# Attention B's output projection: the last group's rows stacked high, high, low for three of four blocks, with its loads moved

## The chip, the core and the metric

The kernel runs on one core of one Trainium2 chip. The time is device microseconds (us) of one launch, from the host's arrays in DRAM to the finished output in DRAM. A shorter time is better.

## The reference, cut to what matters

Two independent attentions, A and B, over S = 2048 positions with D = 576 and 32 heads of Dh = 18 columns each. Their outputs stand side by side, 2048 x 1152.

```python
qkv = x @ wqkv                                   # both A and B, separate weights
# A: each position sees 8 positions, two apart, itself and backwards; softmax; times v
# B: full softmax attention over all 2048 positions
scores = einsum("bhqd,bhkd->bhqk", q, k) * Dh**-0.5
o = einsum("bhqk,bhkd->bhqd", softmax(scores), v)
B = o.transpose(0, 2, 1, 3).reshape(1, S, D) @ wo   # the sum that is changed here
out = concatenate([A, B], axis=-1)
```

What the change touches is the last line for B: 2048 x 576 times 576 x 576, in float32 accuracy.

## The kernel before

**Numbers in halves.** TensorE multiplies in a reduced float32 form here. To keep the accuracy, an operand is kept as a rounded high part and the rest, a low part, and a product is the sum of three: high times high, high times low, low times high. Where the contraction is short, the three products are one instead: the rows are stacked (high, high, low against high, low, high), so that one matmul of 3 x 18 = 54 rows does what three of 18 rows do. The scores of B are made in that way in both kernels (`stack_loads`, line 132).

**B's attention.** The 32 heads are 8 groups `g` of four heads, the 2048 query positions 4 blocks `b` of 512, and the keys 16 tiles `kt` of 128. The main loop (line 1220) takes 8 x 4 x 16 = 512 steps. A step makes the scores of four heads (line 269), their exponentials on ScalarE (line 277), and adds the products with v into the PSUM tile `po` (`weigh`, line 742), one step later. Between these, TensorE makes the maxima of later blocks (line 158), which VectorE reduces (line 166). The maxima of a whole block are turned and written by eight small DMAs (`place`, line 195) into two rows of that block's `qs` tile: `qs<-mh` four times and `qs<-mt` four times. The first score of a block can't start before these have landed. The four maxima of a step run out near step 488 of 512.

**Order.** There is no scheduler: every engine works its instructions in the order in which this Python text issues them. `agenda` maps a step to the functions that are run at its end (`later`, `plan`, `due`, lines 105 to 117). All loads and stores of this stage go through `load`, which is SyncE's (SP's) one DMA queue, in order. In the built program each DMA also waits for the DMA eight places before it in the queue, since eight semaphores are used in turn; so at most eight are under way.

**After a block (`finish`, line 747).** `po` is copied to `o`, its denominators travel to `den`, are inverted on VectorE (line 782), travel back spread out as `rec`, and GpSimd (POOL) multiplies, rounds and subtracts (lines 785 to 787) to get the high and low parts. For groups 0 to 6 these are stored to the DRAM tensor `do`. For group 7, block 0 does this over 26 steps into the tiles `at0` and `at1`; blocks 1 and 2 do it within a few steps with transposes on VectorE instead (`shortly`, line 791); block 3 ends the kernel (`closing`, line 822).

**B's projection.** The weights `wo` of B are five chunks: four of 126 rows, which are 7 heads of groups 0 to 6 each, and one of the four heads of group 7, at rows 0, 32, 64 and 96 of its tile (lines 1151 and 842). Each chunk has a high and a low part. `fetch_old(b)` (line 1011) loads the old rows of block `b`, groups 0 to 6, from `do`: eight DMAs of 252 KB. `full(b, new)` (line 1122) then plans eight quarters: 128 positions times half of the 576 columns. A quarter (`sum_of`, line 1079) runs two rows of sums beside each other, on rows 0 to 63 and 64 to 127 of the array, in two PSUM tiles: five chunks times three products, so 15 pairs of matmuls, 64 x 288 each (line 1071). Quarters go into `inside` (within a step that still has maxima) or `waiting` (between steps). `partial` (line 1138) makes 12 pairs, the old rows only, for three quarters of the positions of block 3.

**Attention A** runs on POOL and VectorE beside the steps (`local`, line 864). Its last outputs, four of them, each go through `together` (line 1175), which does two steps in one with A's projection between (line 1193). Its loads are `at<-dao`, `ahl<-dao` and `aq<-dao`, its stores `dao<-aohi` and `dao<-ao`.

**Steps of group 7** start at 448. There `load_wo` for B's five chunks is planned at 7, 9, 11, 13, 15 (names `y<-wob`; POOL splits each three steps later), `fetch_old(0)` at 4, `fetch_old(1)` at 11, `fetch_old(3)` at 34 and `fetch_old(2)` at 38.

Of the kernel before, what the change touches and what calls it, by code (L numbers as in the profile page):

```python
# [7 lines left out]
F32 = mybir.dt.float32  # L8
F32R = mybir.dt.float32r
# [7 lines left out]
S = 2048  # L17
D = 576
H = 32
DH = 18  # L20
W = 8
DIL = 2
NG = H // 4
NT = S // 128
NB = S // 512
# [4 lines left out]
SUB = AB // 4  # L30
HALO = DIL * (W - 1)

STEPS = NB * NT
# [15 lines left out]
def ap(t, *dims):  # L49

    return bass.AP(tensor=t.tensor, offset=t.offset, ap=[list(t.ap[0])] + [list(d) for d in dims])


def rows(t, *dims):

    return bass.AP(tensor=t.tensor, offset=t.offset, ap=[list(d) for d in dims])
# [3 lines left out]
def two_attentions(ctx: ExitStack, tc, xa, wa, woa, xb, wb, wob, out):  # L60
# [5 lines left out]
    nc = tc.nc  # L66
    load = nc.sync.dma_start

    const = ctx.enter_context(tc.tile_pool(name="const", bufs=1))
    dram = ctx.enter_context(tc.tile_pool(name="dram", bufs=1, space=DRAM))  # L70
# [19 lines left out]
    da = dram.tile([3 * D, HALO + S], F32, name="da")  # L90
    dao = dram.tile([NJ, 2, 4, D, SUB], F32, name="dao")
    drec = dram.tile([NG, NB, 4, 512], F32, name="drec")
    do = dram.tile([2, NG - 1, 128, S], F32, name="do")

    po = p_po.tile([128, 512], F32, name="po")

# [3 lines left out]
    def split_on(engine, hi, lo, raw):  # L100
        engine.tensor_copy(hi, raw)
        engine.tensor_sub(lo, raw, hi)
# [3 lines left out]
    step = 0  # L106

    def later(n, f):
        agenda[step + n].append(f)

    def plan(start, pieces):
        for n, f in pieces:
            agenda[start + n].append(f)
# [6 lines left out]
    sets = []  # L120
# [260 lines left out]
    with (tc.tile_pool(name="x", bufs=1, side="right") as xp,  # L381
# [103 lines left out]
        if True:  # L485
# [9 lines left out]
            chunks = [[(0, 0, 128)], [(0, 128, third - 128), (D, 0, 256 - third)], [(D, 256 - third, 128)]]  # L495
# [185 lines left out]
            for k in range(2, 14):  # L681
                n = 46 if k == 2 else 36 + 4 * k
# [64 lines left out]
    def finish(g, b):  # L747
        o = work.tile([128, 512], F32, name="o", bufs=2)
        if g == NG - 1 and b == NB - 1:
            return closing(b, o, work.tile([128, 512], F32, name="rec", bufs=1))  # L750
        if step + 1 in producing and total - sum(given) >= 8:
            leaving.append(lambda: nc.scalar.activation(o, po, AF.Copy))
        elif step + 1 in producing or sum(given) == total:
            nc.scalar.activation(o, po, AF.Copy)
        else:

            nc.vector.tensor_copy(o, po)
            copied.add(step + 1)
        den = work.tile([128, 16], F32, name="den", bufs=2)
        rec = work.tile([128, 512], F32, name="rec", bufs=1)  # L760
        parts = []

        def room():
            if g == NG - 1 and b == 0:

                parts[:] = [ap(work.tile([128, 4, 128], F32R, name=f"at{i}", bufs=1), (1, 512)) for i in range(2)]
            else:
                n = work.tile([128, 2, 512], F32R, name="n", bufs=1)
                parts[:] = n[:, 0], n[:, 1], n
            return parts  # L770

        if g == NG - 1 and b > 0:
            return shortly(b, o, rec, *room()[:2])

        def store():
            if g < NG - 1:
                load(do[:, g, :, 512 * b : 512 * b + 512].rearrange("i p n -> p i n"), parts[2].bitcast(F32))
            else:
                plan(step, full(b, parts))

        for at, f in ((1, lambda: load(den, o[DH:128:32])),
                      (8, lambda: nc.vector.reciprocal(den, den)),
                      (9, lambda: load(drec[g, b].rearrange("i (p n) -> (i p) n", n=16), den)),
                      (13, lambda: load(rec, rows(drec[g, b], (512, 4), (0, 32), (1, 512)))),
                      (20, lambda: nc.gpsimd.tensor_mul(o, o, rec)),
                      (21, lambda: nc.gpsimd.tensor_copy(room()[0], o)),
                      (22, lambda: nc.gpsimd.tensor_sub(parts[1], o, parts[0])),
                      (26, store)):
            later(at, f)

    def shortly(b, o, rec, hi, lo):

        def halved(cols):
            nc.gpsimd.tensor_copy(hi[:, cols], o[:, cols])
            nc.gpsimd.tensor_sub(lo[:, cols], o[:, cols], hi[:, cols])


        cols = [slice(256 * i, 256 * i + 256) for i in range(2)]
        apart = b == 1
        for i in range(2):  # L800
            later(1 + i * apart, lambda i=i: nc.vector.transpose(rec[:, cols[i]], o[:, cols[i]]))
        later(1 + 2 * apart, lambda: divided(rec))
        for i in range(2):
            later(1 + (3 + i) * apart, lambda i=i: nc.vector.transpose(o[:, cols[i]], rec[:, cols[i]]))
            later(1 + (3 + i) * apart, lambda i=i: halved(cols[i]))
        plan(step, [(at + 2, f) for at, f in full(b, (hi, lo))])

    def inverse(src, turned, cols, o):

# [32 lines left out]
    def load_wo(k, src, *pieces):  # L842

        raw = work.tile([128, D], F32, name="y", bufs=4)
        n = 0
        if len(pieces) == 4:
            nc.gpsimd.memset(raw, 0.0)
            n = 128
        for at, c0, m in pieces:
            load(raw[at : at + m], src[c0 : c0 + m])  # L850
            n = max(n, at + m)
        if k == "a":
            hi = work.tile([128, D], F32R, name="wohi", bufs=5)
            lo = work.tile([128, D], F32R, name="wolo", bufs=5)
        else:

            c = len(wo.get(k, []))
            hi, lo = (ap(t[:, 0, 0, :] if len(t.shape) == 4 else t[:, 0, :], (1, NB * 1024))[:, D * c : D * c + D]
                      for t in sets[(NG - 3) % 3])
        wo.setdefault(k, []).append((hi, lo))  # L860
        later(3, lambda: split_on(nc.gpsimd, hi[:n], lo[:n], raw[:n]))


    def local(j):
# [166 lines left out]
            olds[b].append([t[:n] for t in o])  # L1031


    sums = {}
    ys = {}

# [39 lines left out]
            rings["else"].append(rings["else"].pop(0))  # L1076
        return sums_

    def sum_of(y, t, h, chunks, kind=None):

        pos, cols = slice(128 * t, 128 * t + 128), slice(288 * h, 288 * h + 288)
        both = []
        for r in range(2):
            both.append([])
            for c, (hi, lo) in enumerate(chunks):
                at = slice(64 * r, min(64 * r + 64, hi.shape[0]))
                whi, wlo = wo["b"][c]
                both[r] += [(a[at, pos], w[at, cols]) for a, w in ((hi, whi), (hi, wlo), (lo, whi))]
        one, two = beside(kind, *both)
        if kind:  # L1090
            nc.vector.tensor_copy(y, one)
        else:
            nc.scalar.activation(y, one, AF.Copy)
        nc.vector.tensor_add(y, two, y)
# [24 lines left out]
            half_end(t, b, h, new)  # L1119
        load(out[512 * b + 128 * t : 512 * b + 128 * t + 128, D:], ys[t, b])  # L1120

    def full(b, new):
        def half(t, h):
            if total - sum(given) > 4:
                inside.append(lambda: quarter(t, h, "scores"))
            else:
                waiting.append(lambda: quarter(t, h))

        def quarter(t, h, *kind):
            if h == 0:  # L1130
                ys[t, b] = work.tile([128, D], F32, name="y", bufs=4)
            if h == 1:
                later(1, lambda: load(out[512 * b + 128 * t : 512 * b + 128 * t + 128, D:], ys[t, b]))
            sum_of(ys[t, b][:, 288 * h : 288 * h + 288], t, h, [*olds[b], new], *kind)

        return [(4 + 2 * t + h, lambda t=t, h=h: half(t, h)) for t in range(4) for h in range(2)]

    def partial(t, h):

        b = NB - 1  # L1140
        if h == 0:
            name = ("aq", "ao", "aohi")[t]
            ys["part", t] = work.tile([128, DH, SUB], F32, name=name, bufs=1)
        y = ap(ys["part", t], (1, DH * SUB))[:, 288 * h : 288 * h + 288]
        waiting.append(lambda: sum_of(y, t, h, olds[b]))
        sums[t, b, h] = (y,)

# [8 lines left out]
    for g in range(1, NG):  # L1156
        if g > EARLY:
            plan(STEPS * (g - 2) + 1, [(n, f) for n, f in enumerate(stack_loads(g))])
        if g == NG - 1:
            plan(STEPS * g, [(4, lambda: fetch_old(0)), (11, lambda: fetch_old(1)), (34, lambda: fetch_old(3)),  # L1160
                             (38, lambda: fetch_old(2))])
            plan(STEPS * g, [(n, lambda t=t, h=h: partial(t, h)) for n, (t, h) in
                             zip((43, 44, 45, 47, 49, 51), [(t, h) for t in range(3) for h in range(2)])])
            plan(STEPS * g, [(62, lambda: outside.append(lambda: first(3, NB - 1, 0)))])
            for b in range(NB - 1):
                producing.update(STEPS * g + NT * (b + 1) + (31 if b == 0 else 7) + n for n in range(8))
        plan(STEPS * (g - 1), [(24, lambda g=g: load_v(g))])

    ready = [(0, 0, 0, es)]
# [133 lines left out]
```

## Time and profile before

| | |
|---|---|
| median of 3 runs | 1602.95 us (1602.54 to 1606.55) |
| the profiled execution | 1601.25 us |
| its span in the profile | 1599.4 us |
| mean granted TensorE clock | 0.999 |
| TensorE busy (share of the span) | 1586.0 us (99%) |
| VectorE, ScalarE, GpSimd busy | 1363.5, 1214.4, 959.8 us |
| chain that ended last, TensorE's share | 90% |

The profile shows one execution. Times in it are us from the start of the span; the last step ends about 11 us before its end. PE is TensorE's matmuls, PEld its weight loads, DVE VectorE, ACT ScalarE, POOL GpSimd, SP SyncE. A row of a timeline gives the start, the time taken, the engine, the line of the kernel, the operation with output and input, the number of instructions that are merged in the row, and in brackets how long the engine had been idle before and what ended that. A row of windows gives the busy time of each engine within a stretch, then the granted clock, the mean share of the 16 DMA engines that was busy, and GB/s.

### The profile page before, as it was taken

The page shows a single profiled execution, that of the slowest core. Times are in us where ns is not written, and L with a number is a line of the kernel's source. Part 1 is how long each engine was busy: PE and PEld are TensorE (multiplying, and loading weights), DVE is VectorE, ACT ScalarE, POOL GpSimd, SP SyncE. Part 2 cuts the span into 40 slices and gives each one's busy share as a digit, 9 for nine tenths or more (in the row PEclk, how much of TensorE's full clock was granted, in tenths as well). Part 3 has the DMA queues.
Part 4 walks back from the last instruction along what each step waited for, and adds up shares of the span by engine and source line. Part 5 has one row for each costly group of instructions (what it writes and reads, how often), then busy time and mean ns, then how long its engine had stood idle before and what let it go on. Part 6 is the DMA issues. An engine that isn't in the chain of part 4 may idle for free.

```text
span 1599.4 us, 35014 instructions
## 1 busy us (share of the span) xinstructions
PE 1586.0 (99%) x13324; PEld 964.6 (60%) x13324; DVE 1363.5 (85%) x2315; ACT 1214.4 (76%) x2438; POOL 959.8 (60%) x792
## 2 busy tenths in 40 slices
PE   9999999999999999999999999999999999999998
PEld 7999888999543445444445445445445445545676
DVE  5199999999999999999999999999999999998522
ACT  6423441121699999999999999999999999998655
POOL 2405742210166995995896896797797797772100
PEclk9999999999999999999999999999999999999999
DMA  8937954532212362254326325422732231154111
GB/s 255 233 125 197 275 165 132 147 105 80 61 50 54 80 151 68 55 125 99 74 77 139 78 84 124 105 79 52 143 102 67 61 97 32 44 169 150 70 38 61
DMA packets 186058, 172.10 MB, mean 108 GB/s; under 512 B 119153, under 2 KB 132977, under 8 KB 184161
## 3 DMA queue, kind: packets, MB, share of 16 engines
q1 hardware_dynamic: 181024, 158.31, 36.3%
q0 software_dynamic: 4032, 10.63, 3.2%
q8 instruction: 104, 1.70, 0.5%
q10 hardware_dynamic: 832, 0.92, 0.2%
q14 instruction: 66, 0.53, 0.1%
HBM read 96.94 MB, written 71.90 MB: 106 GB/s over the span
## 4 chain that ended last, share of the span: by engine, by line
PE 90%; DVE 4%; DMA 2%; ACT 2%; POOL 1%; issue 1%; SPq 0%; POOLq 0%; DVEq 0%
PE po L742 28%; PE bank L269 18%; PE bank L158 17%; PE bank L364 14%; PE bank L301 5%; PE bank L1071 4%; PE bank L1193 4%; DVE mx L166 3%; DMA den<-o 1%; ACT e L277 1%; POOL xlo L412 1%; DMA raw<-xa 0%; DMA dqk<-olo 0%; PE bank L516 0%; SPq L509 0%
## 5 line engine op out<-in xcount | busy, mean ns | idle before, releaser
L166 DVE TENSOR_REDUCE mx<-bank 128x2 f32<-128x512 f32 x2048 | 1278.7, 683 | 124.5 <-PE bank L158 91.8
L277 ACT ACTIVATE e<-bank 128x512 f32<-128x512 f32 x2048 | 1046.9, 607 | 66.2 <-PE bank L269 60.3
L158 PE MATMUL bank<-ks,qs 54*128 54x512 f32 (+1 forms) x2466 | 791.3, 382 | 5.8 <-DVE mx L166 4.2
L158 PEld LDWEIGHTS bank<-ks,qs 54*128 54x128 f32 x2466 | 404.0, 184 | 389.1 <-DVE mx L166 340.8
L269 PE MATMUL bank<-qs,ks 56*128 56x512 f32 x2048 | 596.0, 426 | 0.0
L742 PE MATMUL po<-e,v 128*19 128x512 f32 x4096 | 531.5, 599 | 0.0
L269 PEld LDWEIGHTS bank<-qs,ks 56*128 56x128 f32 x2048 | 309.1, 185 | 30.9 <-ACT e L277 24.6
L887 POOL TENSOR_TENSOR pr<-aq,akv 128x1024 f32<-128x1024 f32 x72 | 158.4, 2201 | 15.8 <-DMA akv<-da 13.0
L930 POOL TENSOR_TENSOR pr<-lg,akv 128x1024 f32<-128x1024 f32 x72 | 158.3, 2198 | 0.6
L742 PEld LDWEIGHTS po<-e,v 128*19 128x19 f32 x4096 | 73.9, 97 | 138.0 <-issue 132.6
L891 POOL TENSOR_TENSOR pr<-pr 128x1024 f32<-128x1024 f32 x64 | 152.5, 2383 | 5.0
L692 ACT ACTIVATE ohi<-bank 128x512 f32<-128x512 f32 (+1 forms) x56 | 30.4, 595 | 150.3 <-issue 106.0
L364 PE MATMUL bank<-xhi,ahi 64*128 64x512 f32 (+1 forms) x448 | 113.7, 387 | 0.0
L364 PE MATMUL bank<-xhi,alo 64*128 64x512 f32 (+1 forms) x448 | 110.4, 387 | 0.0
L364 PE MATMUL bank<-xlo,ahi 64*128 64x512 f32 (+1 forms) x448 | 108.1, 388 | 0.1
L1193 PE MATMUL bank<-wohi,at 64*128 64x288 f32 x480 | 103.5, 305 | 0.0
L931 POOL TENSOR_TENSOR pr<-pr 128x512 f32<-128x512 f32 x72 | 92.4, 1284 | 5.6
L412 POOL TENSOR_TENSOR alo<-raw,ahi 128x512 fp32r<-128x512 f32 (+1 forms) x14 | 17.6, 1255 | 123.1 <-ACT ahi L411 101.7
L1193 PEld LDWEIGHTS bank<-wohi,at 64*128 64x128 f32 x480 | 74.8, 184 | 27.5 <-ACT e L277 23.8
L504 POOL TENSOR_TENSOR olo<-olo,ohi 128x512 fp32r<-128x512 f32 x36 | 46.1, 1294 | 63.8 <-ACT ohi L503 60.9
L1193 PE MATMUL bank<-wolo,at 64*128 64x288 f32 x240 | 70.1, 292 | 0.0
L364 PEld LDWEIGHTS bank<-xhi,ahi 64*128 64x128 f32 (+1 forms) x448 | 64.5, 182 | 3.9
(203 smaller groups left out, 1804.9 us busy)
## 6 DMA issues: line engine op xcount, KB each, us to landing
do<-n SPq DMA_DIRECT2D x28, 512.0 KB
da<-ohi SPq DMA_DIRECT2D x52, 256.0 KB
akv<-da SPq DMA_DIRECT2D x64, 175.5 KB
out<-y SPq DMA_DIRECT2D x32, 288.0 KB
qs<-dqk SPq DMA_DIRECT2D x30, 288.0 KB
ks<-dqk SPq DMA_DIRECT2D x30, 288.0 KB
at<-dao SPq DMA_DIRECT2D x60, 128.0 KB
rec<-drec SPq DMA_DIRECT2D x29, 256.0 KB
```

The lines of the kernel that those rows point to most:

```text
L158: return nc.tensor.matmul(ps if part is None else ps[:, 256 * r : 256 * r + 256], qs[at, b, p, 128 * t : 128 * t + 128], ks[at, p, 512 * k ...
L166: nc.vector.tensor_reduce(at, ps.rearrange("q (s n) -> q s n", s=2), axis=AX.X, op=ALU.max)
L269: nc.tensor.matmul(ps, ks[at, p, 128 * kt : 128 * kt + 128], qs[at, b, p], start=True, stop=True)
L277: nc.scalar.activation(e, ps, AF.Exp, scale=SCALE)
L301: nc.tensor.matmul(ps, a, b, start=c == i == 0, stop=c == 4 and i == 1)
L364: nc.tensor.matmul(ps, a, b, start=start, stop=stop)
L742: nc.tensor.matmul(po[32 * i : 32 * i + 19], vs[g][:, kt, 19 * i : 19 * i + 19], es[i], start=kt == 0, stop=kt == NT - 1)
L887: nc.gpsimd.tensor_mul(pr, ap(st["q"][:, 2 * c], (SUB, 2), (0, W), (1, SUB)), window(st["k"], c))
L891: nc.gpsimd.tensor_add(st["pr"], st["pr"], pr)
L930: nc.gpsimd.tensor_mul(at, ap(st["lg"], (0, 2), (SUB, W), (1, SUB)), window(st["v"], c))
L931: nc.gpsimd.tensor_add(at[:, :, :4], at[:, :, :4], at[:, :, 4:])
L1193: return nc.tensor.matmul(ps, a, b, start=r == k == 0, stop=r == 1 and k == len(both[1]) - 1)
```

## The change

For blocks 0, 1 and 2 the new rows (the four heads of group 7) are no longer a fifth chunk with three products. Two stacked tiles per block hold, in each half of the array, the 18 rows of one head as high, high, low (54 rows), and two stacked weight tiles hold high, low, high. A quarter is then 4 x 3 + 2 = 14 pairs of matmuls. Block 3 keeps the old form.

What this needs:

- The high and low parts of group 7 of these blocks are stored to `do` (which has one more group), and `stack_new` loads them back, repeated, with 6 DMAs (blocks 0 and 1, into the tiles `ao` and `aq`) or 8 (block 2, into `at0` and `at1`).
- `load_wo_stack(0)` at step 17 and `(1)` at step 19 of the group: a clearing of a raw tile by POOL, two DMAs of 54 rows that read 18 rows three times, a split by POOL six steps later, and two small DMAs (`qs<-ks`) that put the low part in the middle.
- Block 0's `finish` in group 7 is spread over 16 steps, not 26, and its quarters come before those of block 1; block 1's come 8 steps later than before. The sets of steps in `producing` follow.
- `fetch_old(1)` is planned at 24, not at 11.
- B's weights are split six steps after their load, not three.
- `partial` puts its first two sums in the tiles `wohi` and `wolo`, not `aq` and `ao`.

```diff
-    do = dram.tile([2, NG - 1, 128, S], F32, name="do")
+    do = dram.tile([2, NG, 128, S], F32, name="do")
...
         if g == NG - 1 and b > 0:
-            return shortly(b, o, rec, *room()[:2])
+            return shortly(b, o, rec, *room())
         def store():
             if g < NG - 1:
                 load(do[:, g, :, 512 * b : 512 * b + 512].rearrange("i p n -> p i n"), parts[2].bitcast(F32))
             else:
-                plan(step, full(b, parts))
-
-        for at, f in ((1, lambda: load(den, o[DH:128:32])),
-                      (8, lambda: nc.vector.reciprocal(den, den)),
-                      (9, lambda: load(drec[g, b].rearrange("i (p n) -> (i p) n", n=16), den)),
-                      (13, lambda: load(rec, rows(drec[g, b], (512, 4), (0, 32), (1, 512)))),
-                      (20, lambda: nc.gpsimd.tensor_mul(o, o, rec)),
-                      (21, lambda: nc.gpsimd.tensor_copy(room()[0], o)),
-                      (22, lambda: nc.gpsimd.tensor_sub(parts[1], o, parts[0])),
-                      (26, store)):
+                for i in range(2):
+                    load(do[i, g, :, 512 * b : 512 * b + 512], parts[i].bitcast(F32))
+                later(2, lambda: stack_new(b))
+                plan(step + 2, full(b))
+        times = (1, 8, 9, 13, 20, 21, 22, 26) if g < NG - 1 else (1, 6, 7, 10, 13, 14, 15, 16)
+        for at, f in zip(times, (lambda: load(den, o[DH:128:32]),
...
             later(at, f)
-    def shortly(b, o, rec, hi, lo):
+    def shortly(b, o, rec, hi, lo, both):
...
-        plan(step, [(at + 2, f) for at, f in full(b, (hi, lo))])
+        plan(step, [(6 if apart else 2, lambda: load(do[:, NG - 1, :, 512 * b : 512 * b + 512].rearrange("i p n -> p i n"),
+                                                 both.bitcast(F32))),
+                    (8 if apart else 3, lambda: stack_new(b))])
+        plan(step + (10 if apart else 2), full(b))
...
-        later(3, lambda: split_on(nc.gpsimd, hi[:n], lo[:n], raw[:n]))
+        later(3 if k == "a" else 6, lambda: split_on(nc.gpsimd, hi[:n], lo[:n], raw[:n]))
+    wstack = []
+    def load_wo_stack(p):
+        hi, lo = (ap(t[:, 0, 0, :] if len(t.shape) == 4 else t[:, 0, :], (1, NB * 1024))[:, D * (5 + p) : D * (6 + p)]
+                  for t in sets[(NG - 3) % 3])
+        raw = work.tile([128, D], F32, name="y", bufs=4)
+        nc.gpsimd.memset(raw, 0.0)
+        for r in range(2):
+            load(raw[64 * r : 64 * r + 3 * DH], rows(wob[DH * (H - 4 + r + 2 * p)], (0, 3), (D, DH), (1, D)))
+        wstack.append(hi)
+        later(6, lambda: split_on(nc.gpsimd, hi[:118], lo[:118], raw[:118]))
+        def middle():
+            for r in range(2):
+                at = slice(64 * r + DH, 64 * r + 2 * DH)
+                load(hi.bitcast(F32)[at], lo.bitcast(F32)[at])
+        later(9, middle)
...
+    stacks = {}
+    def stack_new(b):
+        if b < 2:
+            t = ap(work.tile([128, DH, SUB], F32R, name=("ao", "aq")[b], bufs=1), (512, 2), (1, 512))
+            stacks[b] = [t[:, p] for p in range(2)]
+        else:
+            stacks[b] = [ap(work.tile([128, 4, 128], F32R, name=f"at{p}", bufs=1), (1, 512)) for p in range(2)]
+        for i, k, n in ((0, 0, 2), (1, 2, 1)):
+            for r in range(2):
+                at = slice(64 * r + DH * k, 64 * r + DH * (k + n))
+                first = do[i, NG - 1, 32 * r, 512 * b : 512 * b + 512]
+                if b < 2:
+                    for m in range(n):
+                        load(t.bitcast(F32)[at.start + DH * m : at.start + DH * m + DH],
+                             rows(first, (S, DH), (64 * S, 2), (1, 512)))
+                else:
+                    for p in range(2):
+                        load(stacks[b][p].bitcast(F32)[at],
+                             rows(do[i, NG - 1, 32 * r + 64 * p, 512 * b : 512 * b + 512], (0, n), (S, DH), (1, 512)))
...
-    def sum_of(y, t, h, chunks, kind=None):
+    def sum_of(y, t, h, chunks, kind=None, stack=()):
...
+            at = slice(64 * r, 64 * r + 3 * DH)
+            both[r] += [(a[at, pos], w[at, cols]) for a, w in zip(stack, wstack)]
...
-            sum_of(ys[t, b][:, 288 * h : 288 * h + 288], t, h, [*olds[b], new], *kind)
+            sum_of(ys[t, b][:, 288 * h : 288 * h + 288], t, h, olds[b], kind, stacks[b])
...
-            name = ("aq", "ao", "aohi")[t]
-            ys["part", t] = work.tile([128, DH, SUB], F32, name=name, bufs=1)
+            ys["part", t] = (work.tile([128, DH, SUB], F32, name="aohi", bufs=1) if t == 2 else
+                             work.tile([128, D], F32, name=("wohi", "wolo")[t], bufs=5))
...
-            plan(STEPS * g, [(4, lambda: fetch_old(0)), (11, lambda: fetch_old(1)), (34, lambda: fetch_old(3)),
+            plan(STEPS * g, [(4, lambda: fetch_old(0)), (17, lambda: load_wo_stack(0)), (19, lambda: load_wo_stack(1)),
+                             (24, lambda: fetch_old(1)), (34, lambda: fetch_old(3)),
                              (38, lambda: fetch_old(2))])
...
-                producing.update(STEPS * g + NT * (b + 1) + (31 if b == 0 else 7) + n for n in range(8))
+                producing.update(STEPS * g + NT * (b + 1) + (23, 15, 7)[b] + n for n in range(8))
```

More of the change, by code (lines that the diff above doesn't have):

```diff
@@ L778, in store @@
             else:
-                plan(step, full(b, parts))
-        for at, f in ((1, lambda: load(den, o[DH:128:32])),
-                      (8, lambda: nc.vector.reciprocal(den, den)),
-                      (9, lambda: load(drec[g, b].rearrange("i (p n) -> (i p) n", n=16), den)),
-                      (13, lambda: load(rec, rows(drec[g, b], (512, 4), (0, 32), (1, 512)))),
-                      (20, lambda: nc.gpsimd.tensor_mul(o, o, rec)),
-                      (21, lambda: nc.gpsimd.tensor_copy(room()[0], o)),
-                      (22, lambda: nc.gpsimd.tensor_sub(parts[1], o, parts[0])),
-                      (26, store)):
+                for i in range(2):
[4 more added lines that the diff above has]
+        for at, f in zip(times, (lambda: load(den, o[DH:128:32]),
+                                 lambda: nc.vector.reciprocal(den, den),
+                                 lambda: load(drec[g, b].rearrange("i (p n) -> (i p) n", n=16), den),
+                                 lambda: load(rec, rows(drec[g, b], (512, 4), (0, 32), (1, 512))),
+                                 lambda: nc.gpsimd.tensor_mul(o, o, rec),
+                                 lambda: nc.gpsimd.tensor_copy(room()[0], o),
+                                 lambda: nc.gpsimd.tensor_sub(parts[1], o, parts[0]),
+                                 store)):
             later(at, f)
-    def shortly(b, o, rec, hi, lo):
+    def shortly(b, o, rec, hi, lo, both):
         def halved(cols):
@@ L1120, in end, with full @@
         load(out[512 * b + 128 * t : 512 * b + 128 * t + 128, D:], ys[t, b])
-    def full(b, new):
+    def full(b):
         def half(t, h):
@@ L1127, in half, with quarter @@
                 waiting.append(lambda: quarter(t, h))
-        def quarter(t, h, *kind):
+        def quarter(t, h, kind=None):
             if h == 0:
@@ L1141, in partial @@
         if h == 0:
-            name = ("aq", "ao", "aohi")[t]
-            ys["part", t] = work.tile([128, DH, SUB], F32, name=name, bufs=1)
-        y = ap(ys["part", t], (1, DH * SUB))[:, 288 * h : 288 * h + 288]
+            ys["part", t] = (work.tile([128, DH, SUB], F32, name="aohi", bufs=1) if t == 2 else
+                             work.tile([128, D], F32, name=("wohi", "wolo")[t], bufs=5))
+        y = ap(ys["part", t], (1, D))[:, 288 * h : 288 * h + 288]
         waiting.append(lambda: sum_of(y, t, h, olds[b]))
```

## The prediction, made before the changed kernel ran

> **What bounds the kernel now.** I read the page first, then the windows of the last 200 us, then the chain of waits there, then SP's queue, because the change touches only the last group of heads.
>
> ```profile
> span 1599.4 us, 35014 instructions
> PE 90%; DVE 4%; DMA 2%; ACT 2%; POOL 1%; issue 1%; SPq 0%; POOLq 0%; DVEq 0%
> ```
>
> The span is 1599.4 us and the execution it belongs to took 1601.25, so 1.85 us lie around it. The chain is TensorE's for 90%, but that is an average over stages. The windows show the stages:
>
> ```profile
> 1400.00:1425.00 25.00, 25.00 (x199) 10.78 (x196) 23.33 (x40) 24.75 (x49) 23.77 (x25) 1.00 0.48 153
> 1425.00:1450.00 25.00, 23.50 (x184) 9.42 (x182) 21.66 (x36) 23.36 (x47) 13.40 (x13) 1.00 0.56 188
> 1450.00:1475.00 25.00, 25.00 (x246) 17.76 (x242) 21.10 (x39) 18.86 (x40) 2.23 (x4) 1.00 0.41 134
> 1500.00:1525.00 25.00, 25.00 (x293) 18.18 (x287) 4.69 (x11) 15.58 (x34) 0.46 (x2) 1.00 0.08 27
> 1525.00:1550.00 25.00, 25.00 (x303) 18.79 (x301) 5.72 (x14) 13.26 (x30) 2.20 (x4) 1.00 0.09 36
> 1575.00:1600.00 25.00, 18.61 (x180) 14.10 (x176) 7.02 (x18) 10.33 (x24) 1.83 (x4) 0.92 0.19 72
> ```
>
> The columns after the length are PE, PEld, DVE, ACT, POOL, the granted clock, the DMA share and GB/s. Up to 1450 ScalarE is the limit (24.75 of 25 us). From 1450, with A's last four projections, and again from 1500, with B's, PE is busy for all 25 us while DVE and ACT are not: there a matmul that goes is time that goes, and a wait of PE is time lost. In 1425 to 1450 PE misses 1.5 us and ACT 1.6. The chain and the timelines show where:
>
> ```profile
> 1439.08 3.90 DVE L166 TENSOR_REDUCE mx<-bank 128x2 f32<-128x512 f32 x6 [0.16 <-PE bank L158]
> 1443.16 1.89 DVE L166 TENSOR_REDUCE mx<-bank 128x2 f32<-128x512 f32 x3 [0.17 <-PE bank L158]
> 1446.71 0.25 DVE L782 RECIPROCAL den<-den 128x16 f32<-128x16 f32 x1 [1.67 <-DMA den<-o]
> 1448.15 0.38 PE L158 MATMUL bank<-ks,qs 54*128 54x256 f32 x1 [1.50 <-DVE mx L166]
> ...
> 1440.19 6.42 DMA den<-o
> ```
>
> Block 0's denominators land late (6.42 us after their issue), DVE waits 1.67 us for them in front of its reductions, and PE 1.50 us for DVE.
>
> **The pairs.** Each of 24 quarters has 14 pairs of matmuls instead of 15. Nothing else in a quarter goes: still two PSUM tiles, one copy, one addition. Three rows of the chain give the price of a pair:
>
> ```profile
> 1535.39 1.74 PE bank L1071 x24
> 1538.98 2.19 PE bank L1071 x30
> 1544.39 1.77 PE bank L1071 x21
> 1548.01 2.18 PE bank L1071 x28
> ```
>
> A partial (12 pairs, where the view may lose a few records) takes 1.74 to 1.77 us and a quarter (15 pairs) 2.18 to 2.19, so three pairs cost 0.41 to 0.45 us and one about 0.14. [...] 24 x 0.14 = **3.3 us less** (24 x 0.137 to 24 x 0.15: 3.3 to 3.6). 21 of the quarters lie behind 1497, where PE alone works, and three within steps that PE ends. I count all.
>
> **The first stall.** `fetch_old(1)`, eight DMAs of 252 KB, leaves SP's queue ahead of the denominators:
>
> ```profile
> 1421.89 6.81 SPq L1030 DMA_DIRECT2D ks<-do  x8
> 1428.75 1.16 SPq L850 DMA_DIRECT2D y<-wob  x1
> 1429.96 1.16 SPq L784 DMA_DIRECT2D rec<-drec  x1
> 1431.38 2.40 SPq L945 DMA_DIRECT2D dao<-aohi  x1
> 1433.88 3.86 SPq L850 DMA_DIRECT2D y<-wob  x4
> 1440.19 0.60 SPq L781 DMA_DIRECT2D den<-o  x1
> ...
> 1440.18 0.66 POOL L101 CAST qs<-y 126x576 fp32r<-126x576 f32 x1 [8.40 <-DMA y<-wob]
> ...
> SPq L850 <- DMA ks<-do: 2.0, 2, 1.2
> ```
>
> Each of SP's DMAs waits for the one eight places before it, and so the one `y<-wob` after the eight took 1.16 us, and `rec<-drec` as much. Without 6.81 us of issues ahead of it `den<-o` leaves by 1433.4, or by 1434.5 with the two 54-row loads that now also stand there (0.55 each, as the small DMAs below). At 6.42 us of flight, which was the flight behind 2 MB, it has landed by 1440.9. The reciprocal stands six reductions earlier (six times 3.90/6 = 0.65 us, so 3.9): it is due at 1445.05 - 3.9 = 1441.15. The cover is 0.2 us by this bound and some 5 us if the flight is that of an empty queue. I take **1.5 us less up to this point**, the whole wait; both ends 0 and 1.5.
>
> **A wait that comes in its place.** In the changed order SP issues, behind `drec<-den` and from about 1441.8 (1441.15 + 0.25 + 0.35 and a step between), `ks<-do` eight times, and then `do<-n`, `rec<-drec`, the splits `qs<-ks` four times, `qs<-mh` and `qs<-mt` of block 2. The last are eight small DMAs that the first score of block 2 needs.
>
> ```profile
> 1476.00:1491.50 15.50, 15.23 (x152) 8.81 (x144) 14.99 (x29) 11.49 (x23) 4.06 (x6) 1.00 0.45 162
> ...
> 1592.10 2.48 DMA out<-y
> ...
> 1454.65 0.56 SPq L784 DMA_DIRECT2D rec<-drec  x1
> 1456.08 2.28 SPq L195 DMA_DIRECT2D qs<-mh  x4
> 1458.47 2.16 SPq L195 DMA_DIRECT2D qs<-mt  x4
> ...
> 1459.87 1.28 POOL L785 TENSOR_TENSOR o<-o,rec 128x512 f32<-128x512 f32 x1 [3.48 <-DVE mx L166]
> ...
> 1462.26 0.18 PEld L1193 LDWEIGHTS bank<-wohi,aq 64*128 64x128 f32 x1 [0.85 <-DMA qs<-mt]
> ...
> 1463.54 0.39 PE L269 MATMUL bank<-qs,ks 56*128 56x512 f32 x1
> ```
>
> The first row is a stretch in which eight such old rows (`wohi<-do`, `wolo<-do`) are alone on the queues: 162 GB/s, 7.2 of 16 engines. Eight of 252 KB are 2.06 MB, 12.7 us; with a DMA's own 2.5 us (second row) 15.2. The other end is the trace before: the first `ks<-do` was issued at 1421.89, and the loads behind them had reached POOL at 1440.18, 18.3 us later, of which I give the old rows at most 17.2. So they land at 1457.0 to 1459.0; I take 1458.5, nearer the second, since they are the same DMAs. Behind them `do<-n` (512 KB, twice the packets of each, 1.4) and `rec<-drec` (issue to POOL 5.2 us, of which some 2.9 is transfer) end at about 1462.7. That is where the rule of eight bites: five of the small DMAs wait for places taken by `ks<-do`, `do<-n` and `rec<-drec`, and are issued from 1462.7 at 0.55 us each (2.28/4, 2.16/4): the last at 1465, landed 1466.5 (1464.5 to 1468.5 by the ends).
>
> Before, the last of them was issued by 1460.6, and PE took up again at 1462.26, 0.85 us after it had gone idle; the score that is needed began at 1463.54 in the third double step, the third of four there. With the first stall gone it is due at 1462.0. So PE is late by 1466.5 - 1462.0 = 4.5 us, which takes back the 1.5 and adds **3.0 us**; nothing hides it, since from 1450 PE is busy 25.00 of 25. Ends: 1.0 and 5.0 more than before.
>
> [...]
>
> **Block 0's stack.** Its six loads (`ao<-do`) stand behind `do<-at`, eight loads of block 3's or 2's old rows (`pr<-do`, `akv<-do`), and `out`.
>
> ```profile
> 1450.00:1462.00 12.00, 12.00 (x122) 8.63 (x118) 10.66 (x20) 9.51 (x20) 2.23 (x4) 1.00 0.37 108
> ...
> 1461.79 3.21 SPq L1030 DMA_DIRECT2D pr<-do  x4
> 1465.04 3.45 SPq L1030 DMA_DIRECT2D akv<-do  x4
> ...
> 1485.44 0.21 PEld L1071 LDWEIGHTS bank<-qs,n 64*128 64x128 f32 x2
> ```
>
> They were issued from 1461.79, behind the last small DMA; now from about 1467.3 (1465 + `do<-at` and `out`). At 12.7 + 2.5 us they land by 1482.5, by 17.2 at 1484.5; the stack (0.44 MB in thin rows) 2 later, **1484.5 to 1486.5**. It is needed by the last two pairs of the first quarter: now at 1485.44 (the new rows of the first quarter) + 3.0 = 1488.4. So nothing is added; the cover is 1.9 to 3.9 us, and it is the thinnest of the sum.
>
> **Edits costed at nothing.** POOL's two memsets, two splits more and all splits later: POOL is busy 2.23 us of 25 from 1450, and waited 8.40 us for `y<-wob` before; without that cover some 4 us of POOL, none of it PE's. The other stacks, the weights' low rows and block 3's maxima land, by their places in the queue, ten us and more ahead of their use (an estimate), since quarters of block 1 begin 16 steps after those of block 0. Seventeen more SP rows of 0.55 us are 9 us of a queue that stood empty from 1481.8 to 1491.5, by these two rows:
>
> ```profile
> 1481.08 0.71 SPq L1030 DMA_DIRECT2D wolo<-do  x1
> 1491.48 7.98 SPq L1133 DMA_DIRECT2D out<-y  x2
> ```
>
> `partial`'s other tiles and the exchange of the quarters of blocks 0 and 1 move nothing on PE.
>
> **The sum.** -3.3 (pairs) - 1.5 + 4.5 (late `qs<-mt`) = -0.3 us, from 1601.25 to 1601.0 for a profiled execution. The profiled one lies 1.7 us below the median of 1602.95; by the median the forecast is **1602.6 us**.
>
> **Rivals.** *The maxima aren't late.* Small DMAs get past the large ones, or the 2 MB land by 1454. Then -3.3 - 1.5 = -4.8: 1598.1. For it: `qs<-mh` and `qs<-mt` were never seen behind large loads in this trace. Against it: `den<-o` was.
>
> *Block 0's stack comes late: slower.* If `pr<-do` and `akv<-do` move at the 108 GB/s of the window 1450 to 1462, where small DMAs run beside, they take 19 + 2.5 us and the stack lands at 1467.3 + 21.5 + 2 = 1490.8, or 1493 if the maxima are at their late end. PE stands at the stack's pairs from 1488.4, in a stage where it is the limit, 2.4 to 4.6 us: with the sum +2 to +4.5, and with the maxima's late end +6. Taken as +4.5: 1607.5. It decides when the stack lands after 1488.4. For it: thin rows of 2 KB and the longest queue of the kernel. Against it: the 162 GB/s where such loads run alone.
>
> *The clock.* PE idles about 4.5 us at one place. The only 25 us in the trace with so much idle (1575 to 1600) have a granted clock of 0.92, 2.0 us of 25 lost. Here that is up to +2.0: 1604.6. [...]
>
> *A pair costs nothing*, because a quarter is limited by its copies out of PSUM. The rows of 24 and 30 matmuls speak against it. Then +3.0: 1606.0.
>
> **How the numbers follow.** Forecast 0.50; maxima in time 0.20; stack late 0.18; clock 0.06; pairs without gain 0.06. About 0.3%, 4.8 us, is what a measurement of this kernel can tell from no change. Faster by more than that needs the first rival and a little more, half of it and some of unknown gains: 0.14. Slower by more needs 1607.8: half of the late stack, the maxima at their late end with any other: 0.18. Within: 0.68. The range reaches from the first rival's 1598.1, a little below, to the late stack's 1607.5 and 1 us over: 1597.8 to 1608.5.
>
> **What would show it.** The quarters' groups of L1071 have 28 matmuls in about 2.05 us, not 30 in 2.19. The reciprocal on VectorE (L782) has no wait. `ks<-do` starts on SP at about 1441.8, and the last `qs<-mt` is issued near 1465. PE's weight loads wait some 4.5 us for `qs<-mt` in the third double step. The stack's first loads in a quarter (L1071, input `ao`) show no wait for a DMA. The granted clock stays at 1.00 from 1450 to 1550. I am wrong if the small DMAs land while `ks<-do` is under way, if PE waits for `ao<-do`, or if the quarters keep their length.

## The result and the profile after

The changed kernel takes 1606.51 us (median of 17 runs, 1604.75 to 1610.06) against 1602.95 of the kernel before (17 runs, 1600.88 to 1607.26). The ratio is 1.0019, with a 95% interval of 1.0011 to 1.0026: some 3 us slower. The forecast was 0.3 us less: the time lies in its range, but it moved the other way.

The profiled execution has a span of 1604.0 us, 4.6 more than that of before. Executions of all the kernels here differ by up to 4 us at step 448 already, before any instruction that the edits touch, so profiles are compared below from the end of step 448 (1398.82 before, 1399.40 after) to the end of the span: 200.6 us before, 204.6 after. That is +4.0, the part which the change can have made.

These are the windows of the changed kernel (columns as before: PE, PEld, DVE, ACT, POOL, granted clock, DMA share, GB/s).

```profile
1425.00:1450.00 25.00, 25.00 (x199) 10.62 (x197) 23.17 (x40) 24.73 (x50) 18.29 (x20) 1.00 0.55 162
1450.00:1475.00 25.00, 18.43 (x167) 13.89 (x168) 14.92 (x25) 13.61 (x27) 5.08 (x7) 0.86 0.44 159
```

The first row is full now (PE 25.00, not 23.50): the denominators' wait is gone. The second has lost 6.6 us of PE, and its granted clock is 0.86, which it was not before. The timeline around that place, SP's queue first, then VectorE and PE:

```profile
1432.85 0.62 SPq L785 DMA_DIRECT2D den<-o  x1
...
1442.15 0.59 SPq L989 DMA_DIRECT2D aq<-dao  x1
1442.83 1.58 SPq L879 DMA_DIRECT2D y<-wob  x2
1444.52 0.37 SPq L787 DMA_DIRECT2D drec<-den  x1
1444.93 6.20 SPq L1057 DMA_DIRECT2D ks<-do  x8
1451.24 1.48 SPq L777 DMA_DIRECT2D do<-n  x1
1452.77 1.18 SPq L788 DMA_DIRECT2D rec<-drec  x1
1454.05 4.77 SPq L886 DMA_DIRECT2D qs<-ks  x4
1459.60 6.08 SPq L195 DMA_DIRECT2D qs<-mh  x4
1465.78 2.18 SPq L195 DMA_DIRECT2D qs<-mt  x4
...
1441.48 0.24 DVE L786 RECIPROCAL den<-den 128x16 f32<-128x16 f32 x1
...
1459.45 1.91 PE L742 MATMUL po<-e,v 128*19 128x512 f32 x16
1469.33 0.76 PE L269 MATMUL bank<-qs,ks 56*128 56x512 f32 x1 [6.57 <-DMA qs<-mt]
1474.10 1.91 PE L742 MATMUL po<-e,v 128*19 128x512 f32 x16
```

The reciprocal has no bracket: nothing is waited for. Four `qs<-mh` take 6.08 us to issue, where before they took 2.28, and PE stands 6.57 us at the first score that needs them. The chain of waits names what held them:

```profile
1452.77 12.38 DMA rec<-drec
1465.17 0.51 SPq L195
...
1467.45 1.53 DMA qs<-mt
```

`rec<-drec` took 12.38 us from its issue to its landing at 1465.15, behind the eight `ks<-do`, and the fourth `qs<-mh`, which is eight places behind it, was issued at 1465.17. These are the sums with v around the third double step in the kernel before:

```profile
1460.41 1.91 PE L742 MATMUL po<-e,v 128*19 128x512 f32 x16
1466.47 1.91 PE L742 MATMUL po<-e,v 128*19 128x512 f32 x16
```

The third double step lasts 1474.10 - 1459.45 = 14.65 us between its sums with v, against 6.06 before: 8.6 us more, of which 6.57 are the wait. The other 2.0 are the clock, seen in windows of 1 us:

```profile
1466.00:1467.00 1.00, 0.00 (x0) 0.00 (x0) 0.00 (x0) 0.00 (x0) 0.94 (x2) 0.86 0.03 4
1467.00:1468.00 1.00, 0.00 (x0) 0.00 (x0) 0.00 (x0) 0.00 (x0) 0.92 (x2) 0.50 0.02 2
1473.00:1474.00 1.00, 1.00 (x11) 0.94 (x8) 0.84 (x2) 0.77 (x2) 0.00 (x0) 0.72 0.45 137
1474.00:1475.00 1.00, 1.00 (x15) 0.28 (x16) 0.79 (x2) 0.72 (x2) 0.00 (x0) 1.00 0.37 117
```

Half clock from about 1466.7, four microseconds into the wait, to 1473.56, four beyond its end.

The rest is as forecast in kind. Quarters in the chain, and the first loads of block 0's stack:

```profile
1545.36 2.05 PE bank L1120 x28
...
1547.88 2.03 PE bank L1120 x26
...
1493.08 0.36 PEld L1120 LDWEIGHTS bank<-qs,ao 54*128 54x128 f32 x4
```

A quarter (28 matmuls; the view lost two of the second row's) takes 2.05 us where the prediction's rows have 2.18 to 2.19, and the stack's weight loads have no wait. The account, read from the ends of the steps: the denominators -1.56; the third double step +8.60; steps 486 to 509, with the quarters, -2.83; the rest and the end -0.2. Together +4.0.

### The profile page after: what moved, and what is told of

Same layout as the page of the kernel before. It is cut to its first block, busy times and chain, and to the rows that moved or that the text cites. A ratio compares the mean times of both kernels' runs of the same rounds, so it can differ in the third digit from the quotient of the medians.

```text
span 1604.0 us, 34970 instructions
## 1 busy us (share of the span) xinstructions
PE 1585.2 (99%) x13276; PEld 963.5 (60%) x13276; DVE 1363.6 (85%) x2315; ACT 1215.1 (76%) x2438; POOL 965.2 (60%) x798
## 4 chain that ended last, share of the span: by engine, by line
PE 91%; DVE 3%; DMA 2%; ACT 2%; POOL 1%; issue 1%; SPq 0%; POOLq 0%; DVEq 0%
PE po L742 28%; PE bank L269 18%; PE bank L158 17%; PE bank L364 16%; PE bank L301 5%; PE bank L1120 4%; PE bank L1245 3%; DVE mx L166 3%; ACT e L277 1%; DMA den<-o 1%; DMA rec<-drec 1%; POOL xlo L412 1%; PE bank L516 0%; ACT lg L941 0%; DMA out<-y 0%
```

## The experiments

The theory to be tested: the eight loads of block 1's old rows, put at 24, stand ahead of `qs<-mh` and `qs<-mt` in SP's queue; PE waits for these, and the wait drops the clock. Rivals: another of the new loads makes the wait; or a bound that the new rows' stacks set.

**1. The large loads out of the way.**

```diff
-(24, lambda: fetch_old(1)), (34, lambda: fetch_old(3)), (38, lambda: fetch_old(2))
+(36, lambda: fetch_old(1)), (35, lambda: fetch_old(3)), (50, lambda: fetch_old(2))
```

> The changed kernel with its large loads out of the way: the loads of block 1's old rows at 36 (not 24), of block 3's at 35 (not 34, so behind block 0's stack), of block 2's at 50 (not 38, behind the last block's maxima). Theory (the eight loads at 24 make qs<-mt late, and the wait drops the clock): no wait on qs<-mt in the third double step, granted clock 1.00 from 1450 to 1500, the 8.6 us of that double step gone; what is left is 1.5 us less from the denominators and 2.8 less from the pairs, so 4.3 us below the kernel before, about 1598.6 by its median. Rival (the wait has another cause in the changed order, such as the stacked weights' loads or the splits ahead of qs<-mh): the wait on qs<-mt stays at 4 us or more and the time at 1604 or above. Rival (the new rows' stacks become the bound): no wait on qs<-mt, but PE waits for ao<-do or ks<-do, and the time lies between.

Measured: 1597.45 us (5 runs, 1596.04 to 1599.37), ratio to the kernel before 0.9964 (0.9951 to 0.9978). From step 448 to the end 195.9 us, 4.7 less than before (forecast 4.3). Window and SP's queue:

```profile
1450.00:1475.00 25.00, 25.00 (x247) 17.59 (x247) 21.06 (x39) 18.81 (x40) 5.53 (x7) 1.00 0.34 113
...
1455.43 2.32 SPq L195 DMA_DIRECT2D qs<-mh  x4
1457.86 2.18 SPq L195 DMA_DIRECT2D qs<-mt  x4
```

PE has its 25.00 us back and the clock its 1.00; the four `qs<-mh` take 2.32 us again. The stacked weights' loads, the splits and the stacks are all still there, so the order of the old rows' loads makes the wait, and the stacks set no bound. This kernel is faster than both.

**2. Only the move, in the kernel before.**

```diff
-(11, lambda: fetch_old(1))
+(24, lambda: fetch_old(1))
```

> The kernel before with one thing changed: block 1's old rows loaded at 24, not at 11. No stacks, fifteen pairs. Theory: the denominators' wait (1.5 us of PE) goes, and PE waits for qs<-mt in the third double step, somewhat less than the changed kernel's 6.6 us because neither the four splits nor the stacked weights stand in the queue: 3 to 5 us of wait, 0 to 2 us of clock, so 2 to 5.5 us above the kernel before. Rival (the lateness needs the other new loads too): no wait on qs<-mt, and 1.5 us below the kernel before.

Measured: 1606.69 us (10 runs), ratio 1.0022 (1.0013 to 1.0031). The profile has

```profile
1446.19 6.21 SPq L1030 DMA_DIRECT2D ks<-do  x8
1452.50 0.48 SPq L783 DMA_DIRECT2D drec<-den  x1
...
1461.41 0.58 SPq L784 DMA_DIRECT2D rec<-drec  x1
1462.08 2.31 SPq L195 DMA_DIRECT2D qs<-mh  x4
...
1468.05 0.47 PE L269 MATMUL bank<-qs,ks 56*128 56x512 f32 x1 [1.96 <-DMA qs<-mt]
```

Without stacks or new weights PE waits for `qs<-mt` too, so the move is enough. The path is another: here `drec<-den` stands behind the eight loads, where the changed kernel has it ahead of them. It was issued at 1452.50, and `rec<-drec`, which reads what it wrote, at 1461.41, 8.9 us later. The wait, 1.96 us, is shorter than the 3 to 5 expected. The size doesn't close: from step 448 the profile gives 201.5 us, 0.9 more than before, while the runs give +2.1 to +5.0. The profiled execution kept its clock at 1.00 through the wait; experiment 7 shows a wait as short that doesn't. The mean granted clock of each execution is on record: 0.999 in the profiled one, the highest of the ten, and 0.996 to 0.998 in the other nine, where the kernel before has 0.997 to 1.000 in its twenty beside them. A thousandth of 1600 us is 1.6 us, so the eight at 0.996 or 0.997 lost 1.6 us of clock or more that the profiled one kept. That they lost it at this wait fits, but no trace shows the place.

**3. Six of the eight loads at 24**, the other two at 35, and `fetch_old(2)` at 50, in the changed kernel (`fetch_old` takes the chunks as an argument here).

```diff
-(24, lambda: fetch_old(1)),
+(24, lambda: fetch_old(1, range(3))), (35, lambda: fetch_old(1, range(3, 4))),
```

> The changed kernel with six of block 1's eight loads at 24 and the other two at 35 (and block 2's old rows at 50). Theory: each load is 1.53 us of the queue, so qs<-mt lands 3.1 us earlier and PE waits 3.5 us, not 6.6. If the clock falls only when an idle stretch is over some 4 us, as in the changed kernel (idle from 1462.7, half rate from 1466.9), it stays at 1.00 here, the 2.0 us of clock go too, and the time is 5.1 us below the changed kernel; if any long wait costs clock in proportion, half of the 2.0 stays and it is about 4 us below. Rival (qs<-mt waits for something else than these loads): the wait stays at 6 us.

Measured: 1604.00 us (11 runs), ratio 1.0004 (0.9996 to 1.0013); from step 448 201.5 us, 3.15 below the changed kernel.

```profile
1469.13 0.47 PE L269 MATMUL bank<-qs,ks 56*128 56x512 f32 x1 [3.90 <-DMA qs<-mt]
...
1469.00:1470.00 1.00, 0.87 (x8) 0.91 (x9) 0.04 (x1) 0.37 (x1) 0.00 (x0) 0.80 0.99 382
1470.00:1471.00 1.00, 1.00 (x8) 0.99 (x7) 0.65 (x1) 0.72 (x3) 0.00 (x0) 0.50 0.95 310
...
1473.00:1474.00 1.00, 1.00 (x15) 0.52 (x16) 1.00 (x2) 0.84 (x3) 0.00 (x0) 1.00 0.36 127
```

The wait goes with the number of loads (3.90 us, 3.5 expected; 2.67 us less for two loads, 1.3 each and not 1.53). My part on the clock falls in both its forms: the wait was over at 1469.13, before the clock went down at about 1469.6, and 1.65 us were lost all the same (0 or 1.0 forecast).

**4. Block 1's old rows at 11 again**, in the changed kernel.

```diff
-(24, lambda: fetch_old(1))
+(11, lambda: fetch_old(1))
```

> The changed kernel with block 1's old rows loaded at 11 again, as before; all else as changed. Theory: qs<-mt is on time and the 8.6 us go, but den<-o stands behind the eight loads again (landing near 1446) while its reciprocal is due at 1441.5: VectorE waits about 5 us there and PE about as much. So before + 5 - 1.5 - 2.8 = 0.5 us above the kernel before, and up to 2 more if the clock falls in that wait. Rival (the denominators' path was helped by their earlier step and not by the queue): no wait, and 4 us below the kernel before.

Measured: 1610.24 us (5 runs), ratio 1.0039 (1.0027 to 1.0052).

```profile
1424.26 6.26 SPq L1057 DMA_DIRECT2D ks<-do  x8
...
1442.90 3.36 SPq L879 DMA_DIRECT2D y<-wob  x2
1446.97 0.62 SPq L785 DMA_DIRECT2D den<-o  x1
...
1453.30 0.25 DVE L786 RECIPROCAL den<-den 128x16 f32<-128x16 f32 x1 [10.04 <-DMA den<-o]
1454.74 0.58 PE L158 MATMUL bank<-ks,qs 54*128 54x256 f32 x1 [9.89 <-DVE mx L166]
```

The mechanism is right and its size twice what I expected (10.04 us for 5): the queue behind the eight, now with the 54-row loads in it, holds `den<-o` until 1446.97, and its reciprocal is due earlier than before. So the other edits can't have the old place either; the changed place was the better of the two.

**5. Fifteen pairs in the first experiment**: the second stack pair is made twice, so the sums aren't the reference's.

```diff
+            both[r] += both[r][-1:] if stack else []
```

> The kernel with its large loads out of the way (the first experiment), with the second stack pair of each quarter made twice, so fifteen pairs in a quarter as before; the sums are therefore not the reference's. Theory: a pair is worth 0.118 us (2.82 us over 24 quarters between the changed trace and that of before), so the steps from 484 to 509 take 2.8 us longer than with fourteen pairs and nothing else moves: about 1600.3 by the median, 0.18% above the first experiment. Rival (a quarter is limited by its copies): no difference, 1597.5. Rival (the forecast's 0.137 from groups of 24 and 30): 3.3 us.

Measured: 1600.40 us (12 runs), 2.95 above the first experiment; ratio to the kernel before 0.9987 (0.9979 to 0.9996). In the trace steps 486 to 509 take 98.46 us, not 95.51: 2.95 too, 0.123 a pair. The pairs pay, a little under the forecast's 0.137 to 0.15.

**6. Block 2's maxima on POOL's queue.**

```diff
-                    load(ap(qs...), t...)
+                    put = nc.gpsimd.dma_start if g == NG - 1 and b == 2 else load
+                    put(ap(qs...), t...)
```

> The changed kernel with block 2's qs<-mh and qs<-mt issued from POOL's DMA queue, not SP's. Theory (they are late because they stand in SP's queue behind the eight loads, held by the rule of eight and by rec<-drec): POOL issues them right after its split near 1455, they land by 1464 at the latest, and the wait on qs<-mt of 6.6 us falls to 2 us or less, with no clock lost. Rival (the 16 DMA engines themselves are full of the 2 MB, whatever queue the small ones use): they still land after 1466 and the wait stays above 4 us. In either case block 0's stack still lands near 1488 and may be waited for now, since PE reaches it some 8 us earlier.

Measured: 1610.48 us, one run, and no answer to the question: POOL's own multiplication by `rec` stood ahead of these DMAs and waited 9.62 us for `rec<-drec`, so they were issued from 1467.80 and PE waited 10.2 us. It shows that `rec<-drec` behind the eight loads holds POOL as it holds SP. It also bounds the flight of these DMAs from POOL's queue when the eight loads have landed: the last issue ended at 1472.29 and PE was at the scores again from 1473.8, 1.5 us later.

**7. The same, issued ahead of that multiplication** (on top of experiment 6's edit).

```diff
-            later(2 if g == NG - 1 else 5, lambda: place(mh, raw))
+            later(2 if ...) if (g, b) != (NG - 1, 2) else place(mh, raw)
```

> The changed kernel with block 2's qs<-mh and qs<-mt issued from POOL's DMA queue, and right behind POOL's split of them, so ahead of POOL's multiplication that waits for rec<-drec (in the run before, that wait held POOL until 1467.8 and so settled nothing). SP's queue is as changed. Theory (their lateness is SP's queue): issued from 1455.5 to 1460, landed by 1462 to 1464, wait on qs<-mt 0 to 2 us, no clock lost; then PE comes to block 0's stack 7 to 9 us earlier, which lands near 1488 as before, and waits for it 1 to 4 us. Rival (the 2 MB fill the DMA engines whatever queue the small ones stand in): landed after 1466, and the wait stays above 4 us.

Measured: 1600.58 us, one run; from step 448 199.5 us, 5.15 below the changed kernel. POOL's issues, the chain and PE:

```profile
1455.37 2.29 POOL L196 DMA_DIRECT2D qs<-mh  x4
1457.65 2.22 POOL L196 DMA_DIRECT2D qs<-mt  x4
...
1458.75 4.83 DMA qs<-mt
...
1464.59 0.76 PE L270 MATMUL bank<-qs,ks 56*128 56x512 f32 x1 [1.88 <-issue]
...
1464.00:1465.00 1.00, 0.41 (x3) 0.44 (x5) 0.00 (x0) 0.00 (x0) 0.00 (x0) 0.73 0.23 87
...
1467.00:1468.00 1.00, 1.00 (x11) 1.00 (x9) 0.79 (x2) 0.97 (x2) 0.92 (x2) 0.56 0.00 0
```

Most of the wait is SP's queue: it falls from 6.57 to 1.88 us. Of that rest about 0.9 us lie before the last `qs<-mt` landed at 1463.58. These are the large transfers' whatever the queue: 2 KB took 4.83 us to land with them under way. The last landing came 3.7 us after POOL's last issue had ended (1459.87), and from the same queue in experiment 6 at most 1.5 us after it. For the other 1.01 us the profile shows no cause (`issue`). No clock was expected to be lost, but a wait of 1.88 us cost as much of it as that of 3.90. Block 0's stack was not waited for.

**8. Block 3's old rows ahead of block 0's stack again**, in the first experiment (35 to 34).

> The first experiment with block 3's eight loads back at 34, ahead of block 0's stack (ao<-do) in the queue. In the first experiment the stack landed at 1468.5 and was needed near 1484.8. Theory: behind eight loads it lands 14.5 us later, near 1483, so there is still no wait, by 1 to 2 us, and the part from step 448 to the end stays at 195.9 us within 0.3. Rival (the forecast's second rival): it lands after 1484.8 and PE waits for it, 1 to 4 us.

Measured: 1597.38 us, one run; from step 448 195.9 us, and no wait for `ao<-do`. Eight loads ahead of the stack are covered.

**9. Block 1's old rows just behind `qs<-mt`**, in the changed kernel.

```diff
-(24, lambda: fetch_old(1))
+(31, lambda: fetch_old(1))
```

> The changed kernel with block 1's eight old loads at 31, just behind qs<-mt in SP's queue and ahead of block 0's new rows and block 3's old rows. Theory: qs<-mt is on time (landed near 1461) and its wait and clock loss go, but block 0's stack now stands behind sixteen large loads: it lands near 1491, PE needs it near 1484.8, and waits about 6 us, with 1 to 2 us of clock on top; so the part from step 448 to the end is 202 to 204 us, about as in the changed kernel (204.6). Rival (the stack has cover enough): no wait for ao<-do, 195.9 us as in the first experiment.

Measured: 1609.39 us, one run; from step 448 206.1 us.

```profile
1494.63 1.15 PE L1120 MATMUL bank<-qs,ao 54*128 54x288 f32 x4 [7.78 <-DMA ao<-do]
```

The maxima are on time, and PE stands 7.78 us at the stack (6 expected), with half clock behind it. With sixteen loads ahead the forecast's second rival is real; with eight it isn't.

## Why the prediction was wrong

**Right, and shown:** the denominators' wait goes (-1.5 forecast, -1.56). `ks<-do` at 24 delays `qs<-mt`, and PE pays it in the third double step (experiments 1, 2, 3). The last of the eight lands 16 us after their first issue in the changed kernel's trace (forecast 15.2 to 17.2): the second `qs<-mh`, eight places behind it, was issued at 1461.09. The third and the fourth, behind `do<-n` and `rec<-drec` by the rule of eight, were issued at 1462.34 and 1465.17, 1.25 and 2.83 us later, where the forecast's estimates for the two were 1.4 and 2.9. The stack has cover (experiment 8). POOL's extra work costs nothing that shows: in experiment 1 it is all there, and the time from step 448 is 4.7 us less.

**Wrong in size:** "SP issues ... from about 1441.8". I let SP wait for the reciprocal only. The reciprocal came at 1441.48, about as forecast (1441.15), but SP was still at the loads of attention A, and at two `y<-wob` of 54 rows from 1442.83 (the second stacked weights), which this term left out. So `ks<-do` began at 1444.93, 3.1 us later, of which 0.6 is the later start of this execution (step 448). The trace of before held the warning: its reciprocal began at 1446.71, and `drec<-den` left 5 us later, behind the same loads of A.

```profile
1451.04 0.59 SPq L962 DMA_DIRECT2D aq<-dao  x1
1451.72 0.54 SPq L783 DMA_DIRECT2D drec<-den  x1
```

From there the sum holds within 0.7 us: the last `qs<-mt` landed at 1469.0 where I had 1466.5. The wait is 6.57 us, not 4.5: 2.1 us.

**Wrong in kind:** the clock. I saw that PE would idle 4.5 us, priced what that does to the clock at up to 2.0 us, gave that 0.06 as a rival of its own, and let the forecast itself keep the clock at 1.00 from 1450 to 1550. It was 0.86 in 1450 to 1475, and that cost 2.0 us. It is no rival but goes with the forecast's own wait: in the profiled executions, waits of 1.88, 3.90, 6.57, 7.78, 9.89 and 10.2 us all lost clock, and only that of 1.96 us did not. The mean granted clock of all 17 executions of the changed kernel is 0.995 to 0.998, and 0.999 to 1.000 in the five of experiment 1, where the wait is gone. The 0.06 was an estimate that the trace of before couldn't carry: PE's wait there was 1.50 us, the 0.85 us at 1462.26 were its weight loads', under sums with v that ran to 1462.32, and the clock was 1.00 through both. They said nothing of a wait of 4.5.

**Smaller:** the pairs gave 2.83 us, not 3.3 (0.118 each; 0.123 by experiment 5). I took the price from the difference between a quarter and a partial. Two of these rows are whole (30 matmuls in 2.19 us, 24 in 1.74), so lost records aren't the reason; what else differs between the two wasn't looked into. Together: -0.3 + 2.1 + 2.0 + 0.5 = +4.3, against +4.0 in the trace and +3 by the runs (1.8 to 4.2 by the interval).

Of the rivals, "the maxima aren't late" is what experiment 1 makes of the kernel; there its -4.8 is -4.7 in the trace and -5.8 by the runs (-3.5 to -7.9).

## What to carry to other kernels

Before a large load is moved within a queue, write down what stands behind it in the new place and when each of those is due: here the same 2 MB held the denominators in the old place, the maxima in the new one and, with block 3's 2 MB behind it, the stack in a third, and cost nothing only where all that was due soon stood ahead of them. Start such a sum from the queue's own last row before the load, not from the event that seems to release it. A forecast wait on TensorE as long as those that cost clock here has its clock in the price, not in a rival: of seven waits of 1.88 to 10.2 us six cost clock, and the half rate outlasted them by 3 to 5 us.

## What the runs showed of the hardware

The half clock came in multiples of one length. Read from granted clocks in slices of 0.2 us, it lasted 3.41 us in experiments 3 and 7, 6.83 in the changed kernel and in experiment 9, 10.24 in 4 and 13.66 in 6: one, two, three and four times 3.41. It began 1.7 (experiments 6 and 7) to about 5 us (experiments 4 and 9) after PE went idle, so the delay from the stop isn't one figure. This is its end in experiment 9, 4.3 us after PE took up again:

```profile
1498.00:1499.00 1.00, 1.00 (x10) 1.00 (x8) 0.00 (x0) 0.19 (x1) 0.00 (x0) 0.55 0.41 141
1499.00:1500.00 1.00, 1.00 (x17) 1.00 (x16) 0.97 (x2) 1.00 (x3) 0.00 (x0) 1.00 0.45 152
```

So a wait of 1.88 us could lose 1.6 us and one of 1.96 us nothing. What sets the delay, and which stop costs clock, no run here shows.

The rule of eight is in both traces: SP's 1004 DMAs before and 1036 after use eight semaphores, and of the pairs eight places apart 993 of 996 and 1025 of 1028 share one.

That a pair of the stacks costs what another does, as the forecast's 24 x 0.14 takes it, shows in the changed kernel: its matmuls with 288 columns took 293 ns at the median with the 54 rows of `ao`, and 291 to 293 with 62 and 64 rows.
